# VectorE's row sums three banks behind its multiplies, and its sum of the output halves behind the third multiply of the third K part, in a decode attention kernel

## The chip, the cores and the metric

The kernel runs on one core of one Trainium2 chip. The metric is the device time of one execution in microseconds (us), lower is better. The times are the median of several executions; the profile is one further execution, taken by the hardware profiler.

## What is computed

Two attention blocks, A and B, of one form: one new token per sequence (batch 2), 32 heads of 192 numbers, and a cache of 8192 keys and values per head, all bf16. The outputs of the blocks are joined along the last axis.

```python
q = (x @ wq).reshape(B, Sq, H, Dh).transpose(0, 2, 1, 3)
scores = einsum("bhqd,bhkd->bhqk", q, k_cache) * (Dh ** -0.5)
p = softmax(scores, axis=-1)
o = einsum("bhqk,bhkd->bhqd", p, v_cache)
return o.transpose(0, 2, 1, 3).reshape(B, Sq, H * Dh) @ wo
# x (2, 1, 640), k_cache and v_cache (2, 32, 8192, 192), wq (640, 6144), wo (6144, 640)
```

Every key and value is used once, so the caches are read once from the chip's memory, and there is little arithmetic for each byte.

## The kernel before

**Units and parts.** The work is cut into 16 units (`NU`): a block, a sequence and a group of 8 heads. The keys of a unit are spread over 128 partitions, each with 512 tokens of one head (`TP`), and so are the values. Both are loaded in 3 parts (`NCH`) of 64 KB per partition, 8.39 MB a part. Three buffers in `big` (`NBUF`) hold them in turn. The list `loads` gives the order: K parts 0 to 2 of the first unit, then in turns V part c of unit u-1 and K part c of unit u, and last the three V parts of the last unit. All loads stand in one queue that SyncE issues (`ld_kv`, waits at L504 to L506): load i waits until the load three before it has been used up (`done`, L495), a K part by the last of its sums on TensorE ("sl"), a V part by its last product on TensorE ("pv"). So a K load waits for a "pv", and a V load for an "sl".

**A K part** has 170 whole tokens. VectorE multiplies them in place by the query (`dve_mul`, L303), in 5 instructions (`NSUB`) that are called m0 to m4 here: four of 32 tokens (6144 numbers per partition) and one of 42 (8064). Tokens that are cut by a part's edge are multiplied into `pad` (L301). TensorE then adds the 192 products of a token down to 16 with 12 matmuls against an identity, 32 tokens to a PSUM bank (`pe_sum`, L420, called s0 to s4); there are three such banks, `scps0` to `scps2`, taken in turn (`bank`, L306). VectorE adds the last 16 of a bank (`dve_red`, L311, called r0 to r4) into the scores `sc`. The ten tokens that are over go to a bank of their own (`pe_rest`, L432), which VectorE adds once for a unit (`dve_rest`, L315). A sum s waits for its multiply, and for the r of the bank's user three sums ago (`prev`, L559).

**Softmax.** After the last r of the third part VectorE takes the row maximum, GpSimd the maximum over partitions, ScalarE the exponential, and VectorE spreads the probabilities into `pb` (`dve_spread`, L338).

**A V part** is 85 matmuls of 384 columns and one or two small ones (`pe_pv`, L450 and L456), called pv0 to pv2, all three into the one bank `ops`. Its two halves (tokens of even and odd number) are then added, and divided by the sum of the exponentials: VectorE's reciprocal (L347), copy (L350) and sum (L353), then ScalarE (L356) and one matmul (L462) that places the eight rows. The function `turn_out` records the three steps of VectorE and ScalarE's.

**Order.** The program writes out by hand, unit by unit, what each engine does in which order (`put`, L566, and the loop at L569); each engine goes strictly in its order, and waits of semaphores stand between the engines. Within a unit u and part c, TensorE does pv c of the unit before (v = u - 1), and then s0 to s4 of K part c. VectorE does the multiplies of K part c, with the row sum of the bank before behind each. `turn_out` stands ahead of the third part's multiplies. Unit 0 has no V work, and after the last unit the loop goes once more with V work alone. Units from 1 on run as a hardware loop.

Of the kernel before, what the change touches and what calls it, by code (L numbers as in the profile page):

```python
# [119 lines left out]
def build_kernel(nc, blocks, out):  # L120
# [10 lines left out]
    NCH = 3  # L131
# [5 lines left out]
    NSUB = TC // SUB  # L137
# [18 lines left out]
    with ExitStack() as es:  # L156
# [135 lines left out]
        def dve_su(u):  # L292
            return lambda eng: eng.tensor_tensor(su[:], esel[:], onehot[:, S_dve.at(u)].broadcast_to([128, 144]), ALU.mult)  # L293

        def dve_mul(u, c, k):
            b = buf["k", u, c]

            def fn(eng):
                if k == 0:
                    for t, lo, hi, src in fragments(b, c):  # L300
                        eng.tensor_tensor(pad[:, t, lo:hi], src, qt[:, 0, lo:hi], ALU.mult)  # L301
                t = tokens(b, c, SUB * k, size(k))
                return eng.tensor_tensor(t, t, qt[:].broadcast_to([128, size(k), Dh]), ALU.mult)  # L303
            return fn
# [4 lines left out]
        def dve_red(u, c, k):  # L309
            lo = TC * c + SUB * k  # L310
            return lambda eng: eng.tensor_reduce(sc[:, lo:lo + SUB], scps[bank(u, c, k)][:], AXL.X, ALU.add)  # L311
# [18 lines left out]
        def dve_spread(ranges):  # L330
            dst = pb[:].rearrange("p (g a j h) -> p g a j h", a=2, j=4, h=UH)
            src = sc[:].rearrange("p (g j a) -> p g a j", j=4, a=2)

            def fn(eng):
                for lo, hi in ranges:
                    for a in range(2):
                        shape = [128, hi - lo, 4, UH]
                        ins = eng.tensor_tensor(dst[:, lo:hi, a], src[:, lo:hi, a].unsqueeze(3).broadcast_to(shape),  # L338
                                                mask[:].unsqueeze(1).unsqueeze(1).broadcast_to(shape), ALU.mult)
                return ins  # L340
            return fn
# [73 lines left out]
        def pe_sum(u, c, k):  # L415
            t = tokens(buf["k", u, c], c, SUB * k, SUB)

            def fn(eng):
                for j in range(NJ):
                    ins = eng.matmul(scps[bank(u, c, k)][:], ident[:], t[:, :, j * DG:(j + 1) * DG],  # L420
                                     start=(j == 0), stop=(j == NJ - 1))
                return ins
            return fn

        def pe_rest(u, c):
            t = tokens(buf["k", u, c], c, SUB * NSUB, REST)
            parts = [(REST * c, REST, t)] + ([(NCH * REST, 2, pad[:])] if c == NCH - 1 else [])

            def fn(eng):
                for lo, n, src in parts:  # L430
                    for j in range(NJ):
                        ins = eng.matmul(rest[:, lo:lo + n, :], ident[:], src[:, :, j * DG:(j + 1) * DG],  # L432
                                         start=(j == 0), stop=(j == NJ - 1))
                return ins
            return fn
# [7 lines left out]
        def pe_pv(u, c):  # L443
            b = buf["v", u, c]

            def fn(eng):
                for j in range(TC // 2):
                    j0 = col(TC * c + 2 * j)
                    last = c == NCH - 1 and j == TC // 2 - 1
                    ins = eng.matmul(ops[0:MP, 0:QW], pb[:, j0:j0 + MP],  # L450
                                     bufs[b][:, OFF[c] + j * QW:OFF[c] + (j + 1) * QW],
                                     start=(c == 0 and j == 0), stop=last, skip_group_check=True)
                    if j == 0:
                        for t, lo, hi, src in fragments(b, c):
                            j0 = col(NCH * TC + t)
                            eng.matmul(ops[0:UH, lo:hi], pb[:, j0:j0 + UH], src, start=False, stop=False,  # L456
                                       skip_group_check=True)
                return ins
            return fn

        def pe_pl(u):
            return lambda eng: eng.matmul(oacc_all[:, 0:Dh], place[:, S_pe.at(UH * u, 128, UH)], o_sb[:],  # L462
                                          start=False, stop=True, skip_group_check=True)
# [95 lines left out]
        def prev(u, c, k):  # L559
            n = u * NCH * NSUB + c * NSUB + k - 3  # L560
            return ("r", n // (NCH * NSUB), n // NSUB % NCH, n % NSUB) if n >= 0 else None
# [4 lines left out]
        def put(eng, slot, name, fn, waits, lag=0):  # L566
            slots[eng].setdefault(slot, []).append((name, fn, [w for w in waits if w is not None], lag))

        for u in range(NU + 1):  # L569
            real, old = u < NU, u >= 1  # L570
            v = u - 1

            def red(c, k):
                put("dve", u, ("r", c, k), dve_red(u, c, k), [("s", u, c, k), ("sp", u - 1) if u else None])

            def turn_out():
                put("dve", u, ("rc", -1), dve_rc, [("pv", v, NCH - 1), ("of", v - 1)])
                put("dve", u, ("oh", -1), dve_ohi, [("of", v - 1)])
                put("dve", u, ("os", -1), dve_osum, [("oh", v)])
                put("act", u, ("of", -1), act_of, [("os", v), ("rc", v), ("pl", v - 1)])  # L580

            def v_part(c):
                if c == 0:
                    put("pe", u, ("l", -1), pe_l, [("exp", v), ("sp0", v), ("os", v - 1), ("rc", v - 1)])
                put("pe", u, ("pv", c, -1), pe_pv(v, c), [("v", v, c), ("sp", v) if c else None])

            if not real:
                for c in range(NCH):
                    v_part(c)
                turn_out()  # L590
                put("pe", u, ("pl", -1), pe_pl(v), [("of", v)])
                continue
            put("dve", u, ("su", 1), dve_su(u + 1), [("q", u)])
            for c in range(NCH):
                if old:
                    v_part(c)
                if old and c == NCH - 1:
                    turn_out()
                for k in range(NSUB):
                    w = [("k", u, c), ("qe", u), ("sl", u - 1, NCH - 1) if u and c == 0 else None]  # L600
                    put("dve", u, ("m", c, k), dve_mul(u, c, k), w)
                    put("pe", u, ("s", c, k), pe_sum(u, c, k), [("m", u, c, k), prev(u, c, k)])
                    if old and c == NCH - 1 and k == 0:
                        put("pe", u, ("pl", -1), pe_pl(v), [("of", v)])
                    if k:
                        red(c, k - 1)
                    elif c:
                        red(c - 1, NSUB - 1)
                put("pe", u, ("sl", c), pe_rest(u, c),
                    [("m", u, c, NSUB - 1), ("rl", u - 1) if u and c == 0 else None])  # L610
            c = NCH - 1
            red(c, NSUB - 1)
            put("dve", u, ("rl",), dve_rest, [("sl", u, c)])
            put("dve", u, ("mx",), dve_max, [("rl", u)])
            put("dve", u, ("mp",), dve_mp, [("mx", u), ("ar", u - 1) if u else None, ("negm",)])
            put("dve", u, ("nm",), dve_nm, [("ar", u)])
            put("dve", u, ("nb",), dve_nb, [("nm", u), ("exp", u - 1) if u else None])
            put("pe", u, ("q", 1), pe_q, [("su", u + 1), ("qe", u)])
            put("pool", u, ("ar",), pool_ar, [("mp", u), ("nm", u - 1) if u else None])
            put("act", u, ("qe", 1), act_q, [("q", u + 1), ("m", u, NCH - 1, NSUB - 1)])  # L620
            put("act", u, ("exp",), act_exp, [("nb", u), ("l", v) if u else None])
            g0, g1 = -(-TC // 8), TP // 8
            put("dve", u, ("sp0",), dve_spread([(0, g0), (g1 - 1, g1)]),
                [("exp", u), ("pv", v, NCH - 1) if u else None, ("mask",)])
            put("dve", u, ("sp",), dve_spread([(g0, g1 - 1)]), [])
# [107 lines left out]
```

## Time and profile before

| | |
|---|---|
| median of 3 executions | 1964.3 us |
| the executions | 1964.3, 1970.02 and 1940.62 us |
| the profiled execution | 1947.18 us, its span 1945.5 us |
| mean granted TensorE clock in it | 0.938 of full speed |
| TensorE busy (matmuls) | 1533.6 us, 79% of the span |
| VectorE busy | 1121.8 us, 58% |
| ScalarE, GpSimd busy | 30.1 us, 8.8 us |
| DMA | 836.98 MB, 430 GB/s over the span |

In the lines of the profile, PE is TensorE, PEld its weight loads, DVE VectorE, ACT ScalarE, POOL GpSimd, and SP SyncE, which issues all the loads. A row of the timeline has the start in us, the duration in us, the engine, the line and the operation, its count, and in brackets how long the engine had stood idle before it and what it waited for. A row of the groups has a count, the busy time in us and the mean in ns of one, and the idle time ahead. In a row of the DMA issues the last number is the time in us from issue to landing; it contains the wait behind loads issued earlier. A row of the windows gives the busy us of each engine in that stretch, then the granted clock (PEclk), the busy share of the 16 DMA engines and the bytes moved.

### The profile page before, as it was taken

Reading aid. Unit: us, or ns where it says so; the run is one execution under the profiler, and the core shown is the slowest. Engines: PE = TensorE matmul, PEld = TensorE weight load, DVE = VectorE, ACT = ScalarE, POOL = GpSimd, SP = SyncE. Lnnn points to the kernel's source line nnn. Section 1 sums busy time; section 2 is a strip of 40 time slices with the busy share of each in tenths; the row PEclk is TensorE's granted clock in tenths of the full one; section 3 lists DMA queues with packets and bytes.
Section 4 is the critical chain, followed back from the end, with each engine's and each line's share of the span. In section 5 each row is a group of like instructions: output and inputs, shape, how many; then the busy total and the mean of one; then the engine's idle time right before and its main releaser. Section 6 shows DMA issues by size and latency. Waiting matters only on the chain.

```text
span 1945.5 us, 18505 instructions
## 1 busy us (share of the span) xinstructions
PE 1533.6 (79%) x8255; PEld 780.4 (40%) x8256; DVE 1121.8 (58%) x835; ACT 30.1 (2%) x76; POOL 8.8 (0%) x60
## 2 busy tenths in 40 slices
PE   5678778887977878778787977978788787977979
PEld 3234344333433434344343433434344343433435
DVE  0786555665556475555765557476565656556450
ACT  0000000000000000000000000000000000000000
POOL 0000000000000000000000000000000000000000
PEclk9899889899999989999899999989999998999989
DMA  9999999999999999999999999999999999999998
GB/s 428 433 429 431 429 435 435 433 433 437 424 431 431 431 431 431 431 431 431 434 434 438 433 435 431 434 433 431 433 435 434 434 435 434 433 434 431 431 433 345
DMA packets 15149, 836.98 MB, mean 430 GB/s; under 512 B 1688, under 2 KB 1824, under 8 KB 2208
## 3 DMA queue, kind: packets, MB, share of 16 engines
q1 hardware_dynamic: 15136, 836.78, 99.5%
q8 instruction: 11, 0.18, 0.0%
q14 instruction: 2, 0.02, 0.0%
HBM read 836.77 MB, written 0.01 MB: 430 GB/s over the span
## 4 chain that ended last, share of the span: by engine, by line
PE 54%; DVE 30%; issue 14%; DMA 2%; another core or an unknown queue 0%; POOL 0%; ACT 0%; DVEq 0%; SPq 0%; ACTq 0%; POOLq 0%
PE ops L450 34%; DVE big L303 23%; PE scps L420 16%; DVE sc L311 3%; PE rest L432 2%; DMA big<-in_B_wq_dram 2%; DVE pb L338 1%; PE scps L402 1%; DVE rmax L319 1%; PE outps L484 0%; PE ops L456 0%; PE scps L484 0%; POOL mg L344 0%; DVE o_hi L350 0%
## 5 line engine op out<-in xcount | busy, mean ns | idle before, releaser
L420 PE MATMUL scps<-big,ident 128*128 128x512 bf16 x2880 | 728.5, 410 | 298.7 <-DVE big L303 298.7
L303 DVE TENSOR_TENSOR big<-big,qt 128x6144 bf16<-128x6144 bf16 (+1 forms) x240 | 850.2, 3548 | 0.0
L450 PE MATMUL ops<-big,pb 128*40 128x384 bf16 x4080 | 706.8, 335 | 0.0
L420 PEld LDWEIGHTS scps<-big,ident 128*128 128x128 bf16 x2880 | 281.8, 104 | 729.7 <-DVE big L303 376.6
L450 PEld LDWEIGHTS ops<-big,pb 128*40 128x40 bf16 x4080 | 412.9, 102 | 270.0 <-issue 24.7
L311 DVE TENSOR_REDUCE sc<-scps 128x32 f32<-128x512 f32 x240 | 164.5, 685 | 265.8 <-PE scps L420 265.8
L347 DVE RECIPROCAL rc<-ops 8x1 f32<-8x1 f32 x16 | 2.5, 156 | 322.3 <-PE ops L450 322.3
L301 DVE TENSOR_TENSOR pad<-big,qt 128x128 bf16<-128x128 bf16 (+1 forms) x64 | 11.5, 200 | 135.0 <-DMA big<-in_A_k_cache_dram 68.9
L338 DVE TENSOR_TENSOR pb<-sc,mask 128x704 bf16<-128x704 f32 (+2 forms) x96 | 76.3, 863 | 14.1 <-ACT sc L366 14.1
L438 PE MATMUL ops<-rs,mask 128*8 128x1 f32 x32 | 3.1, 167 | 84.8 <-DVE pb L338 84.8
L432 PE MATMUL rest<-big,ident 128*128 128x160 bf16 x576 | 47.7, 233 | 0.0
L432 PEld LDWEIGHTS rest<-big,ident 128*128 128x128 bf16 x576 | 42.7, 98 | 12.1 <-issue 1.8
L438 PEld LDWEIGHTS ops<-rs,mask 128*8 128x8 f32 x32 | 1.6, 90 | 88.4 <-DVE pb L338 82.8
L402 PE MATMUL scps<-big,pb 128*64 128x384 bf16 x160 | 28.5, 343 | 2.4 <-DMA big<-in_B_wq_dram 1.9
L356 ACT ACTIVATE o_sb<-o_hi,rc 8x192 bf16<-8x192 f32 x16 | 7.3, 454 | 1357.7 <-DVE o_hi L353 1357.7
L402 PEld LDWEIGHTS scps<-big,pb 128*64 128x64 bf16 x160 | 18.4, 116 | 12.3 <-DMA big<-in_B_wq_dram 2.3
L293 DVE TENSOR_TENSOR su<-esel,onehot 128x144 bf16<-128x144 bf16 x17 | 5.1, 301 | 28.7 <-PE outps L410 28.7
L394 PE MATMUL rest<-ident,pb 4*128 4x4 bf16 x5 | 0.4, 178 | 21.5 <-DMA pb<-in_B_x_dram 21.5
L315 DVE TENSOR_REDUCE sc<-rest 128x30 f32<-128x480 f32 x16 | 10.5, 657 | 6.9 <-PE rest L432 6.9
L344 POOL PARTITION_ALL_REDUCE mg<-mp x16 | 5.8, 366 | 1866.9 <-DVE mp L322 1866.9
L359 ACT ACTIVATE qt<-outps 128x192 bf16<-128x192 f32 x17 | 5.6, 330 | 455.6 <-PE outps L410 455.6
L366 ACT ACTIVATE sc<-sc,nb 128x512 f32<-128x512 f32 x16 | 11.5, 721 | 32.8 <-DVE nb L328 32.8
(66 smaller groups left out, 125.6 us busy)
## 6 DMA issues: line engine op xcount, KB each, us to landing
big<-in_B_wq_dram SPq DMA_DIRECT2D x1, 7680.0 KB, 37.2
big<-in_A_wo_dram SPq DMA_DIRECT2D x1, 7680.0 KB, 24.3
big<-in_A_wq_dram SPq DMA_DIRECT2D x1, 7168.0 KB, 20.2
big<-in_B_wo_dram SPq DMA_DIRECT2D x1, 4640.0 KB, 21.2
big<-in_B_wo_dram SPq DMA_DIRECT2D x1, 1760.0 KB, 25.1
big<-in_B_wo_dram SPq DMA_DIRECT2D x1, 800.0 KB, 26.6
big<-in_A_wq_dram SPq DMA_DIRECT2D x1, 512.0 KB, 3.8
big<-in_A_k_cache_dram SPq DMA_DIRECT2D x24, 29.9
```

The source lines that it names most:

```text
L301: eng.tensor_tensor(pad[:, t, lo:hi], src, qt[:, 0, lo:hi], ALU.mult)
L303: return eng.tensor_tensor(t, t, qt[:].broadcast_to([128, size(k), Dh]), ALU.mult)
L311: return lambda eng: eng.tensor_reduce(sc[:, lo:lo + SUB], scps[bank(u, c, k)][:], AXL.X, ALU.add)
L315: eng.tensor_reduce(dst, rest[:, 0:NCH * REST, :].rearrange("p (c t) g -> p c t g", c=NCH), AXL.X, ALU.add)
L319: return eng.tensor_reduce(rmax[:], sc[:], AXL.X, ALU.max)
L338: ins = eng.tensor_tensor(dst[:, lo:hi, a], src[:, lo:hi, a].unsqueeze(3).broadcast_to(shape), mask[:].unsqueeze(1).unsqueeze(1).broadcast ...
L356: return eng.activation(o_sb[:], o_hi[:], ACTF.Identity, scale=rc[:])
L366: return eng.activation(sc[:], sc[:], ACTF.Exp, bias=nb[:], scale=scale, accum_out=rs[:])
L402: ins = eng.matmul(flat[blk][64 * blk:64 * blk + 64, 0:QW], xz[:, blk, c, XM - m:XM - m + 64], wq_t[blk][:, c, QW * m:QW * m + QW], start= ...
L420: ins = eng.matmul(scps[bank(u, c, k)][:], ident[:], t[:, :, j * DG:(j + 1) * DG], start=(j == 0), stop=(j == NJ - 1))
L432: ins = eng.matmul(rest[:, lo:lo + n, :], ident[:], src[:, :, j * DG:(j + 1) * DG], start=(j == 0), stop=(j == NJ - 1))
L450: ins = eng.matmul(ops[0:MP, 0:QW], pb[:, j0:j0 + MP], bufs[b][:, OFF[c] + j * QW:OFF[c] + (j + 1) * QW], start=(c == 0 and j == 0), stop= ...
```

## The change

In the order of VectorE's work three things move; no operation is added or taken away, and nothing is changed in what is computed, in the loads, or in their order.

1. Row sum number n of a unit (n counts its 15 banks) stood behind the multiply n + 1; it now stands behind the multiply n + 3. The last three row sums of a unit stand together behind its last multiply, where one stood alone.
2. `turn_out` (reciprocal, copy and sum of the output halves) stood ahead of the third part's m0; it now stands ahead of its m3, behind the row sum that follows m2.
3. On TensorE the matmul that places the output rows (L462) stood behind s0 of the third part, and now stands behind s3.

```diff
             for c in range(NCH):
                 if old:
                     v_part(c)
-                if old and c == NCH - 1:
-                    turn_out()
                 for k in range(NSUB):
+                    if old and c == NCH - 1 and k == 3:
+                        turn_out()
                     w = [("k", u, c), ("qe", u), ("sl", u - 1, NCH - 1) if u and c == 0 else None]
                     put("dve", u, ("m", c, k), dve_mul(u, c, k), w)
                     put("pe", u, ("s", c, k), pe_sum(u, c, k), [("m", u, c, k), prev(u, c, k)])
-                    if old and c == NCH - 1 and k == 0:
+                    if old and c == NCH - 1 and k == 3:
                         put("pe", u, ("pl", -1), pe_pl(v), [("of", v)])
-                    if k:
-                        red(c, k - 1)
-                    elif c:
-                        red(c - 1, NSUB - 1)
+                    n = NSUB * c + k - 3
+                    if n >= 0:
+                        red(n // NSUB, n % NSUB)
                 put("pe", u, ("sl", c), pe_rest(u, c),
                     [("m", u, c, NSUB - 1), ("rl", u - 1) if u and c == 0 else None])
             c = NCH - 1
-            red(c, NSUB - 1)
+            for k in range(NSUB - 3, NSUB):
+                red(c, k)
```

On VectorE, at the start of a unit (K part 0) in the loop, before; `128x6144` and `128x8064` are multiplies, `sc<-scps0` is the row sum of the first bank, and the rows of L110 compute the number that the next semaphore wait needs:

```order
L303 TENSOR_TENSOR big<-big,qt 128x6144 x2
L110 REGISTER_ALU
L110 ISA
L311 TENSOR_REDUCE sc<-scps0 128x32
L303 TENSOR_TENSOR big<-big,qt 128x6144
L110 REGISTER_ALU
L311 TENSOR_REDUCE sc<-scps1 128x32
L303 TENSOR_TENSOR big<-big,qt 128x6144
L110 REGISTER_ALU
L311 TENSOR_REDUCE sc<-scps2 128x32
L303 TENSOR_TENSOR big<-big,qt 128x8064
```

The same place with the change:

```order
L303 TENSOR_TENSOR big<-big,qt 128x6144 x4
L110 REGISTER_ALU
L110 ISA
L311 TENSOR_REDUCE sc<-scps0 128x32
L303 TENSOR_TENSOR big<-big,qt 128x8064
L110 REGISTER_ALU
L311 TENSOR_REDUCE sc<-scps1 128x32
```

Four multiplies, where there were two, now stand ahead of the first instruction that needs a sum of TensorE's.

On VectorE, at the start of the third K part, before:

```order
L347 RECIPROCAL rc<-ops 8x1
L350 COPY o_hi<-ops 8x192
L110 REGISTER_ALU
L353 TENSOR_TENSOR o_hi<-ops,o_hi 8x192
L301 TENSOR_TENSOR pad<-big,qt 128x128
L303 TENSOR_TENSOR big<-big,qt 128x6144
L311 TENSOR_REDUCE sc<-scps0 128x32
```

With the change, from the third part's m2 on:

```order
L303 TENSOR_TENSOR big<-big,qt 128x6144
L110 REGISTER_ALU
L311 TENSOR_REDUCE sc<-scps0 128x32
L110 REGISTER_ALU
L347 RECIPROCAL rc<-ops 8x1
L350 COPY o_hi<-ops 8x192
L110 REGISTER_ALU
L353 TENSOR_TENSOR o_hi<-ops,o_hi 8x192
L303 TENSOR_TENSOR big<-big,qt 128x6144
L110 REGISTER_ALU
L311 TENSOR_REDUCE sc<-scps1 128x32
L303 TENSOR_TENSOR big<-big,qt 128x8064
```

The reciprocal, which waits for pv2, stood ahead of the part's `pad` and m0, and now stands behind its m2; the row sum ahead of it is that of the last bank of the part before.

On VectorE, from the last multiply of a unit on, with the change (before, one row sum stood behind the one that follows the last multiply, where three stand now):

```order
L303 TENSOR_TENSOR big<-big,qt 128x8064
L110 REGISTER_ALU
L311 TENSOR_REDUCE sc<-scps2 128x32
L110 REGISTER_ALU
L311 TENSOR_REDUCE sc<-scps0 128x32
L110 REGISTER_ALU
L311 TENSOR_REDUCE sc<-scps1 128x32
L110 REGISTER_ALU
L311 TENSOR_REDUCE sc<-scps2 128x32
L110 REGISTER_ALU
L315 TENSOR_REDUCE sc<-rest 128x3x10
```

The last sum on TensorE (s4, in `scps2`) now waits for the first of these four, since it stands in the same bank.

## The prediction

> **What bounds the kernel now.** I read the page's slices and queues first, then the windows, the waits, the DMA issues, and one unit of the timeline.
>
> ```profile
> span 1945.5 us, 18505 instructions
> PE 1533.6 (79%) x8255; PEld 780.4 (40%) x8256; DVE 1121.8 (58%) x835; ACT 30.1 (2%) x76; POOL 8.8 (0%) x60
> DMA  9999999999999999999999999999999999999998
> GB/s 428 433 429 431 429 435 435 433 433 437 424 431 431 431 431 431 431 431 431 434 434 438 433 435 431 434 433 431 433 435 434 434 435 434 433 434 431 431 433 345
> q1 hardware_dynamic: 15136, 836.78, 99.5%
> ```
> ```profile
> 15.00:1915.00 1900.00, 1507.23 (x7986) 765.08 (x7987) 1118.66 (x824) 26.41 (x66) 5.85 (x16) 0.94 1.00 433
> 1938.00:1945.50 7.50, 5.71 (x86) 3.48 (x80) 0.48 (x1) 0.43 (x1) 0.00 (x0) 1.00 0.01 3
> ```
>
> No engine is busy all the time, but the transfers are: between 15 and 1915 us the DMA share is 1.00 at 433 GB/s, and the one queue's packets fill 99.5% of the span. Only the last 7.5 us, the end of the output product and its store, move nothing. The time is the bytes: 836.78 MB at 433 GB/s are 1932.5 us, and a start and an end lie around them. The chain of waits puts most of its shares on TensorE and VectorE, but that tells only who released the last instruction; it isn't a bound while loads are queued.
>
> So the question is whether the queue ever runs dry, and by how little it doesn't. The groups and one unit:
>
> ```profile
> L303 DVE TENSOR_TENSOR big<-big,qt 128x6144 bf16<-128x6144 bf16 x192 | 641.4, 3348 | 0.0
> L303 DVE TENSOR_TENSOR big<-big,qt 128x8064 bf16<-128x8064 bf16 x48 | 208.8, 4349 | 0.0
> L311 DVE TENSOR_REDUCE sc<-scps 128x32 f32<-128x512 f32 x240 | 164.5, 685 | 265.8 <-PE scps L420 265.8
> L347 DVE RECIPROCAL rc<-ops 8x1 f32<-8x1 f32 x16 | 2.5, 156 | 322.3 <-PE ops L450 322.3
> ```
> ```profile
> 1062.82 0.33 SPq L254 DMA_DIRECT2D big<-in_B_v_cache_dram  x1
> 1083.95 0.33 SPq L254 DMA_DIRECT2D big<-in_B_k_cache_dram  x1
> 1086.75 0.69 DVE L311 TENSOR_REDUCE sc<-scps 128x32 f32<-128x512 f32 x1 [8.80 <-PE scps L420]
> 1087.36 3.35 DVE L303 TENSOR_TENSOR big<-big,qt 128x6144 bf16<-128x6144 bf16 x1
> ...
> 1091.23 3.35 DVE L303 TENSOR_TENSOR big<-big,qt 128x6144 bf16<-128x6144 bf16 x1
> ...
> 1107.88 0.29 DVE L301 TENSOR_TENSOR pad<-big,qt 128x64 bf16<-128x64 bf16 x2 [7.83 <-DMA big<-in_B_k_cache_dram]
> ...
> 1117.30 0.33 SPq L254 DMA_DIRECT2D big<-in_B_k_cache_dram  x1
> 1120.01 0.69 DVE L311 TENSOR_REDUCE sc<-scps 128x32 f32<-128x512 f32 x1 [4.70 <-PE scps L420]
> ...
> 1132.75 4.40 PE L420 MATMUL scps<-big,ident 128*128 128x512 bf16 x12 [2.10 <-DVE big L303]
> ...
> 1138.02 0.33 SPq L254 DMA_DIRECT2D big<-in_B_v_cache_dram  x1
> ...
> 1138.34 13.83 PE L450 MATMUL ops<-big,pb 128*40 128x384 bf16 x84
> 1152.20 0.16 DVE L347 RECIPROCAL rc<-ops 8x1 f32<-8x1 f32 x1 [18.90 <-PE ops L450]
> ...
> 1153.05 0.20 DVE L301 TENSOR_TENSOR pad<-big,qt 128x128 bf16<-128x128 bf16 x1
> ...
> 1173.80 2.77 PE L420 MATMUL scps<-big,ident 128*128 128x512 bf16 x12 [2.10 <-DVE big L303]
> ...
> 1177.71 0.33 SPq L254 DMA_DIRECT2D big<-in_B_v_cache_dram  x1
> ...
> 1183.15 0.20 PE L438 MATMUL ops<-rs,mask 128*8 128x1 f32 x2 [5.29 <-DVE pb L338]
> 1199.42 0.33 SPq L254 DMA_DIRECT2D big<-in_B_k_cache_dram  x1
> ```
>
> Two of VectorE's waits are of the kernel's own making. Its row sums stand 265.8 us in all: at 1086.75 and at 1120.01 a row sum waits (8.80 and 4.70 us) until TensorE, busy with a V part, comes to the first sum, and the multiplies behind it wait too. The reciprocal stands 322.3 us: at 1152.20 it has waited 18.90 us for pv2.
>
> What these waits cost the queue is read from when loads are issued. Four of the issues, asked for by time:
>
> ```profile
> big<-in_B_v_cache_dram SPq DMA_DIRECT2D x1, 25.7
> ...
> big<-in_B_k_cache_dram SPq DMA_DIRECT2D x1, 23.9
> ```
> ```profile
> 502.16 0.33 SPq L254 DMA_DIRECT2D big<-in_A_k_cache_dram  x1
> 523.01 0.33 SPq L254 DMA_DIRECT2D big<-in_A_v_cache_dram  x1
> ```
> ```profile
> big<-in_A_k_cache_dram SPq DMA_DIRECT2D x1, 22.6
> ```
> ```profile
> big<-in_A_v_cache_dram SPq DMA_DIRECT2D x1, 21.8
> ```
>
> The V load issued at 1062.82 lands 25.7 us later, at 1088.5. The K load behind it is issued at 1083.95, so 4.6 us before that, and lands at 1107.9, 19.3 us after it: a part takes 19.3 us, and six parts, one unit, 116 us. In the other pair the first lands at 524.8, and the second, issued 1.75 us before, at 544.8: 20.0 us later, so about 0.7 us were lost. From these a load must be issued some 2.45 us (1.75 + 0.7, an estimate) before the one ahead lands. The margin of the unit shown is then 4.6 - 2.45 = 2.1 us in 116. The loop of compute is nearly as long as that of the transfers, but shorter.
>
> **The change, part by part.** No bytes, no instructions of VectorE or TensorE and no matmuls are added or removed; the work moves in order.
>
> *Multiplies ahead of the row sum.* By the rows at 1087.36 and 1091.23 a multiply and a row sum take 3.87 us together. K part 1 lands at 1107.88. With the change, m0, m1 and m2, each with an old row sum that is long ready, begin at 1108.1 and end with their row sums at 1119.7; m3 ends at 1123.0; r0 doesn't wait, since pv1 ends at 1117.3 and s0, 2.8 us long, at 1120.1. m4 ends at about 1127.9 (4.3 us), r1 at 1128.6, and s4, which now waits for r1 in the same bank, begins at 1128.7, where it began at 1132.75. That is 4.0 us earlier; s4 also ran slowly there (4.40 us; 2.77 in the row at 1173.80), so up to 5.6 us. The new wait of s4 costs 0.69 us in each part (one row sum), included here; behind it are only the rest's matmuls and the next pv.
>
> *The output halves behind m2.* K part 2, issued at 1117.30, lands about two parts behind part 1, at 1107.9 + 38.7 = 1146.6. Before, its `pad` begins at 1153.05. With the change the three pairs fill 1146.8 to 1158.4; pv2, some 5 us earlier by the step ahead, has long ended, so the three small steps (0.85 us, 1152.20 to 1153.05) don't wait; m3 with its row sum takes to 1163.1, m4 to 1167.4, r1 to 1168.1. s4 begins at 1168.2, not 1173.80: 5.6 us earlier. r2 and r3 fit under it, r4 follows it as before. What is behind keeps its distances, so pv0 begins at about 1177.6, where it began at 1183.15, and the K load goes out at 1193.8, where it went at 1199.42. Bounds: 6.45 us if nothing else came late (1153.05 - 1146.6), and none at all if VectorE found part 2 landing only after pv2. I take 5.6, as its three pieces are all read from rows.
>
> *The moved matmul of L462* goes from behind s0 to behind s3, and its cost, a quarter of a microsecond on TensorE, stays; ScalarE's step ahead of it ends about 1.1 us after the halves are added, before m3 is done. Nothing waits for it within the unit.
>
> *What all this is worth.* The slack per unit goes from 2.1 to about 7.7 us, and in place of VectorE's waits for TensorE stand waits for landings. No part lands earlier for it while the queue never ran dry. What is won is what did run dry: in the page's slices under 431 GB/s (428, 429, 429, 424; the last apart) 14 of 431 are missing from a slice of 48.6 us, so 1.6 us in all. The lower bound is the 0.7 of the one late load.
>
> [...]
>
> The sum: the profiled execution took 1947.2 us, of which 1945.5 are its span; less 1.6 us that makes **1945.6 us**. The median of the three shown is 1964.3, but they reach from 1940.62 to 1970.02, and the profiled one is among the lower. The forecast says that executions of the changed kernel lie at the transfers' own time. A slower one before would then be one whose loop of compute was longer: 17.1 us above the profiled one (1964.3 - 1947.2) are 1.1 us for each of 15 units with V work, for which the loop must have grown 2.1 + 1.1 = 3.2 us of 116; the changed order holds 7.7.
>
> **Rivals.** *A: the transfers make the spread.* If slower executions are slower because the memory delivers less, the loop of compute has nothing to do with it, and the change nothing to give: about 1964 us, within 1950 to 1972. For it: the trace shown has hardly a gap, so it can't say what a slow one looks like. Against it: the rate between gaps is steady (431 to 438 in nearly all slices), and the margin is just thin enough to be lost.
>
> *B: slower, by TensorE's clock.* The sums now come in bursts, and TensorE stands idle longer between landings:
>
> ```profile
> 1178.00:1182.00 4.00, 0.00 (x0) 0.00 (x0) 2.52 (x7) 1.12 (x3) 0.36 (x1) 0.81 1.10 475
> 1182.00:1186.00 4.00, 2.85 (x11) 1.38 (x12) 4.00 (x7) 0.00 (x0) 0.00 (x0) 0.50 0.99 426
> 1187.00:1199.00 12.00, 12.00 (x74) 7.35 (x73) 5.86 (x2) 0.00 (x0) 0.00 (x0) 0.99 1.01 437
> ```
>
> After an idle stretch (no matmul from 1178 to 1182) the granted clock was 0.50, and 0.99 some microseconds later. If the clock stayed at half through a whole pv0, its 13.8 us would be 27.7, some 12 us above the 16.3 that it takes now with its slow start; that is beyond the 7.7 us by 4.3 us a unit, and 15 units make 65 us: about 2010 us. It decides from about 24 us for pv0 (16.3 + 7.7). Against it: the clock recovers within 4 us. [...]
>
> *C: faster by over 2%.* From 1964.3 that is below 1925.8, less than the bytes take at 433 GB/s with the ends around them; it needs a bad run of before beside a good one of after.
>
> *D: the row sums wait all the same*, now at landings, and sums come no earlier: if K parts landed too late for four multiplies to be done under pv0, the wait of 8.80 us would move and not go. The time would be that of the forecast or 1947.2, as the queue is full either way.
>
> **How the numbers follow.** The forecast, with D in it, has 0.67, its own range 1939 to 1950. A has 0.26, B 0.03, C 0.04. The range, 1938 to 1967, takes in most of A. A measurement of this kernel tells about 2% from no change. Forecast and A are both within it, so within 2% has 0.93; faster by more has C's 0.04, slower by more B's 0.03.
>
> **What the profile after would show.** Right: the share of q1 at 99.5% or above; VectorE's idle time ahead of L311 far under 265.8 us and ahead of L347 near zero, with idle time ahead of L301 on DMA grown well over the present waits; K loads issued some 10 us before the landing ahead, where 4.6 was shown; longer times to landing. All executions would lie near 1945. Wrong: slices with a DMA digit under 9 or under 424 GB/s; a granted clock well under 0.938 with pv0 above 24 us; or executions spread to 1964 as before with the queue full, which would be A.

## The result, and the profile after

The median is 1940.5 us over 20 executions (1940.16 to 1941.10), where the kernel before, in 20 executions beside it, had 1964.28 (1940.39 to 1970.02). The ratio of after to before is 0.9927, with a 95% interval of 0.9899 to 0.9955: 0.7% faster, clear of noise and within the 2% that the forecast spoke of. The profiled execution took 1940.39 us (before 1947.18).

The forecast was 1945.6 us, its own range 1939 to 1950, the whole range 1938 to 1967. More striking than the median is the spread: under 1 us after the change, 30 us before it.

From the page of the changed kernel, the span, the transfer rate per slice, the queue, and three groups (busy us, mean ns, then the idle time ahead and who ended it):

```profile
span 1938.7 us, 18520 instructions
GB/s 416 440 432 434 432 433 434 433 433 433 433 434 433 433 433 433 435 435 433 435 434 433 433 433 433 433 433 434 434 434 434 435 433 434 433 433 433 434 432 381
q1 hardware_dynamic: 15136, 836.78, 99.8%
...
L301 DVE TENSOR_TENSOR pad<-big,qt 128x128 bf16<-128x128 bf16 (+1 forms) x64 | 11.9, 206 | 649.5 <-DMA big<-in_B_k_cache_dram 343.1
L311 DVE TENSOR_REDUCE sc<-scps 128x32 f32<-128x512 f32 x240 | 160.8, 679 | 26.6 <-PE scps L420 26.6
...
L347 DVE RECIPROCAL rc<-ops 8x1 f32<-8x1 f32 x16 | 2.3, 147 | 42.7 <-PE ops L450 42.7
```

From the third slice on, the slices have 432 to 435 GB/s (the last apart); the dip to 424 is gone. VectorE's row sums wait 26.6 us where they waited 265.8. The reciprocal's 42.7 us are one wait, that of the last unit, where VectorE has nothing else to do. What VectorE waits for now is K parts landing, 649.5 us ahead of L301: it is ahead of the transfers.

The first line of section 4 of the two pages, the chain of work that ended last by engine, tells the same; before first, then after:

```profile
PE 54%; DVE 30%; issue 14%; DMA 2%; another core or an unknown queue 0%; POOL 0%; ACT 0%; DVEq 0%; SPq 0%; ACTq 0%; POOLq 0%
```
```profile
DMA 43%; PE 25%; DVE 19%; issue 12%; DVEq 0%; POOL 0%; ACT 0%; SPq 0%; ACTq 0%; POOLq 0%
```

Transfers have 2% of the chain before and 43% after.

One unit of the changed kernel in the timeline, to set beside the unit in the prediction:

```profile
1105.30 0.29 DVE L301 TENSOR_TENSOR pad<-big,qt 128x64 bf16<-128x64 bf16 x2 [19.94 <-DMA big<-in_B_k_cache_dram]
...
1125.98 4.45 PE L420 MATMUL scps<-big,ident 128*128 128x512 bf16 x12 [2.10 <-DVE sc L311]
...
1143.99 0.23 DVE L301 TENSOR_TENSOR pad<-big,qt 128x128 bf16<-128x128 bf16 x1 [18.07 <-DMA big<-in_B_k_cache_dram]
...
1155.74 0.15 DVE L347 RECIPROCAL rc<-ops 8x1 f32<-8x1 f32 x1
...
1165.43 2.76 PE L420 MATMUL scps<-big,ident 128*128 128x512 bf16 x12 [1.92 <-DVE sc L311]
...
1169.35 0.33 SPq L254 DMA_DIRECT2D big<-in_B_v_cache_dram  x1
...
1182.83 13.16 DVE L303 TENSOR_TENSOR big<-big,qt 128x6144 bf16<-128x6144 bf16 x4
1190.62 0.33 SPq L254 DMA_DIRECT2D big<-in_B_k_cache_dram  x1
```
```profile
big<-in_B_v_cache_dram SPq DMA_DIRECT2D x1, 32.7
```

The reciprocal at 1155.74 has no wait ahead of it. The V load issued at 1169.35 lands 32.7 us later, at 1202.0; the K load behind it goes out at 1190.62, 11.4 us before that. In the unit of before that the prediction shows, a K load went out 4.6 us ahead.

### The profile page after: what moved, and what is told of

Read it like the earlier page. It is cut to its first block, busy times and chain, and to the rows that moved or that the text cites. A ratio compares the mean times of both kernels' runs of the same rounds, so it can differ in the third digit from the quotient of the medians.

```text
span 1938.7 us, 18520 instructions
## 1 busy us (share of the span) xinstructions
PE 1518.8 (78%) x8255; PEld 781.2 (40%) x8256; DVE 1118.8 (58%) x835; ACT 30.1 (2%) x76; POOL 8.8 (0%) x60
## 4 chain that ended last, share of the span: by engine, by line
DMA 43%; PE 25%; DVE 19%; issue 12%; DVEq 0%; POOL 0%; ACT 0%; SPq 0%; ACTq 0%; POOLq 0%
DMA big<-in_A_k_cache_dram 20%; DMA big<-in_B_k_cache_dram 19%; PE ops L450 18%; DVE big L303 15%; PE scps L420 4%; DVE sc L311 3%; DMA big<-in_B_wo_dram 2%; PE rest L432 1%; DMA pb<-in_B_x_dram 1%; PE scps L402 1%; DVE pb L338 1%; DVE rmax L319 0%; PE ops L456 0%; POOL mg L344 0%; DVE o_hi L350 0%
## 5 line engine op out<-in xcount | busy, mean ns | idle before, releaser
L420 PE MATMUL scps<-big,ident 128*128 128x512 bf16 x2880 | 713.5, 405 | 305.4 <-DVE sc L311 283.1
L450 PE MATMUL ops<-big,pb 128*40 128x384 bf16 x4080 | 704.0, 334 | 0.0
L420 PEld LDWEIGHTS scps<-big,ident 128*128 128x128 bf16 x2880 | 282.1, 103 | 720.2 <-DVE sc L311 361.1
L450 PEld LDWEIGHTS ops<-big,pb 128*40 128x40 bf16 x4080 | 411.7, 102 | 268.3 <-issue 22.0
L301 DVE TENSOR_TENSOR pad<-big,qt 128x128 bf16<-128x128 bf16 (+1 forms) x64 | 11.9, 206 | 649.5 <-DMA big<-in_B_k_cache_dram 343.1
L311 DVE TENSOR_REDUCE sc<-scps 128x32 f32<-128x512 f32 x240 | 160.8, 679 | 26.6 <-PE scps L420 26.6
L432 PEld LDWEIGHTS rest<-big,ident 128*128 128x128 bf16 x576 | 45.2, 102 | 15.3 <-issue 7.0
L432 PE MATMUL rest<-big,ident 128*128 128x160 bf16 x576 | 49.6, 238 | 0.0
L347 DVE RECIPROCAL rc<-ops 8x1 f32<-8x1 f32 x16 | 2.3, 147 | 42.7 <-PE ops L450 42.7
```

The lines of the kernel that those rows point to most:

```text
L450: ins = eng.matmul(ops[0:MP, 0:QW], pb[:, j0:j0 + MP], bufs[b][:, OFF[c] + j * QW:OFF[c] + (j + 1) * QW], start=(c == 0 and j == 0), stop= ...
```

## Where the 6.8 us between the two profiled executions lie

The last K load, its landing, and the end of the kernel: the issue rows and the times to landing, before and then after.

```profile
1813.62 0.33 SPq L254 DMA_DIRECT2D big<-in_B_k_cache_dram  x1
...
1880.32 15.60 PE L450 MATMUL ops<-big,pb 128*40 128x384 bf16 x85
...
1926.91 8.36 PE L484 MATMUL outps<-big,oT 128*2 128x320 bf16 x96
...
1943.75 0.43 ACT L386 ACTIVATE pb<-scps 2x320 bf16<-2x320 f32 x1 [8.02 <-PE scps L484]
```
```profile
big<-in_B_k_cache_dram SPq DMA_DIRECT2D x1, 29.6
```
```profile
1799.84 0.33 SPq L254 DMA_DIRECT2D big<-in_B_k_cache_dram  x1
...
1872.26 16.69 PE L450 MATMUL ops<-big,pb 128*40 128x384 bf16 x85
...
1919.94 6.68 PE L484 MATMUL outps<-big,oT 128*2 128x320 bf16 x96
...
1929.29 5.89 PE L484 MATMUL scps<-big,oT 128*2 128x320 bf16 x80 [0.83 <-DMA big<-in_B_wo_dram]
1935.44 1.48 PE L484 MATMUL scps<-big,oT 128*2 128x320 bf16 x16 [0.26 <-DMA big<-in_B_wo_dram]
1936.96 0.43 ACT L386 ACTIVATE pb<-scps 2x320 bf16<-2x320 f32 x1 [9.87 <-PE scps L484]
```
```profile
big<-in_B_k_cache_dram SPq DMA_DIRECT2D x1, 40.7
```

The last K part lands at 1843.2 before and at 1840.5 after: the transfers ran dry about 2.7 us less. Before, nearly all of it was lost at five loads that went out 1.8 to 3.6 us ahead of the landing before them. From that landing to the first matmul of the last unit's pv0 it takes 37.1 us before (to 1880.32) and 31.8 after (to 1872.26), 5.3 us less. That is the shortening of the third part which the prediction worked out as 5.6, but here, in the last unit, no further K load stands behind it: three V products and the output product follow on TensorE one after another, and they end the kernel. Together the last pv0 begins 8.1 us earlier, and the last evacuation (L386) 6.8. In between, a slower pv0 (16.69 against 15.60) costs 1.1 us; the first of the two output products gains 1.7 (6.68 against 8.36); and the second ends with 1.9 less of a lead, of which 1.1 are waits for the last pieces of the output weights (0.83 and 0.26), for which TensorE now arrives too early.

This divides the 6.8 us at the landing; it doesn't show that earlier landings alone would have saved 2.7, since the last unit of before follows TensorE's own order of work and not the landing, as is worked out below. Nor is the end of before always longer: its fastest executions (1940.15 to 1940.5 us) are as short as those of the changed kernel.

## The experiments

In all of them before is timed beside. Its executions there lay between 1940 and 1956 us, save one at 2307, with medians of 1945.1 to 1945.7; the group from 1964 to 1970 was seen in the first timing alone. The experiments come from three rounds, each on another chip, and the chip of the first timing isn't on record. So differences of a microsecond between runs of different rounds mean little, and that the long group belongs to one chip isn't ruled out.

**Each part of the change alone.** `e2_lag_only` undoes this of the change (the diff is against the changed kernel):

```diff
+                if old and c == NCH - 1:
+                    turn_out()
                 for k in range(NSUB):
-                    if old and c == NCH - 1 and k == 3:
-                        turn_out()
...
-                    if old and c == NCH - 1 and k == 3:
+                    if old and c == NCH - 1 and k == 0:
                         put("pe", u, ("pl", -1), pe_pl(v), [("of", v)])
```

> Only the row sums move three banks back; the sum of the output halves stays ahead of the third part's first multiply. Theory L, both parts do the same job: part 1's sums end 4 to 5.6 us earlier, so the third V part ends about when the third K part lands and the reciprocal hardly waits; the slack is some 6 to 7 us and all executions lie near 1941. Rival, the reciprocal ahead of the third part is what ties VectorE to TensorE: the slack stays near 2 us and the times stay in two groups, median 1944 to 1965.

Measured 1942.02 us (1940.45 to 1942.23), 0.9969 of before (0.9955 to 0.9984).

`e3_turn_only` undoes the rest:

```diff
-                    n = NSUB * c + k - 3
+                    n = NSUB * c + k - 1
...
-            for k in range(NSUB - 3, NSUB):
-                red(c, k)
+            red(c, NSUB - 1)
```

> Only the sum of the output halves (and its placing matmul) moves behind the third part's third multiply; the row sums stay one multiply behind. Theory L: the third part's multiplies begin at its landing, some 6 us earlier, of which about 1 us goes to the wait for its first sum; slack about 6 us, all executions near 1941. Rival, the row sums are what matters: slack near 2 us, two groups as before, median 1944 to 1965.

Measured 1940.48 us (1940.18 to 1940.89), 0.9972 of before (0.9957 to 0.9987). VectorE's waits in the two, the row sums moved alone and then the output halves alone:

```profile
DVE rc L347 <- PE ops L450: 326.1, 16, 41.3
...
DVE sc L311 <- PE scps L420: 50.6, 25, 3.4
```
```profile
DVE sc L311 <- PE scps L420: 153.7, 51, 8.2
DVE rc L347 <- PE ops L450: 41.7, 1, 41.7
```

Either part takes its own wait away or most of it (the row sums' 265.8 us become 50.6, the reciprocal's 322.3 become the 41.7 of the last unit) and leaves most of the other's, and either is enough to free the transfers. Both rivals, by which only one of the two matters, fell. But the way that was expected for the first did not come: with the row sums moved alone the reciprocal waits 326.1 us, as long as before, and not hardly. What it gains in the first two parts is enough, as it seems. The two do the same job, so their gains don't add: moving the output halves alone has all of it, and the row sums alone all but 1.5 us.

**How much slack there is.** In the next kernels VectorE takes further row maxima of the scores in each unit, into a tile that nothing reads, ahead of the one that counts; they stand in the path from the third K part to pv0. In the trace 8 of them take 4.8 us.

```diff
+        dose = sb("dose", [128, 8], F32)
...
         def dve_max(eng):
+            for i in range(8):
+                eng.tensor_reduce(dose[:, i:i + 1], sc[:], AXL.X, ALU.max)
             return eng.tensor_reduce(rmax[:], sc[:], AXL.X, ALU.max)
```

> The changed kernel with 8 more row maxima of the scores per unit, written to a place that nothing reads, ahead of the one that counts: by the pace of row sums in a row (0.62 us each) some 5 us more in the path from the third K part to the first V product. Theory L: the slack of 8.9 us per unit (loads go out 11.4 us before the landing ahead, less 2.45) holds it: time near 1940.5, issues 6.4 us ahead of the landing instead of 11.4. Theory T: the same time, as nothing but transfers counts. If the slack were used up otherwise: 5 us for each of 16 units, near 2020.

Measured 1943.01 us (1942.33 to 1946.98). The 4.8 us in each of 16 units, 77 us of work, cost 2.5 us in all. Nothing was expected, and a bound by compute would give some 80. In the loop the K loads of the second part go out 5.2 to 5.8 us ahead of the landing, where 6.4 was expected. Two kernels tell where the 2.5 us are, with the same row maxima in all units but the last, and in the last alone. The diff is against the kernel ahead; its last change takes the last unit out of VectorE's hardware loop, so that it can differ:

```diff
-        def dve_max(eng):
-            for i in range(8):
-                eng.tensor_reduce(dose[:, i:i + 1], sc[:], AXL.X, ALU.max)
-            return eng.tensor_reduce(rmax[:], sc[:], AXL.X, ALU.max)
+        def dve_max(u):
+            def fn(eng):
+                for i in range(8 if u < LASTU else 0):
+                    eng.tensor_reduce(dose[:, i:i + 1], sc[:], AXL.X, ALU.max)
+                return eng.tensor_reduce(rmax[:], sc[:], AXL.X, ALU.max)
+            return fn
...
-                S_dve.emit(eng, [(1, NU, 1)])
+                S_dve.emit(eng, [(1, LASTU, 1)])
```

> The changed kernel with the 8 further row maxima (4.8 us in the trace of the run ahead) in all units but the last, whose instructions stand outside the hardware loop. Theory E (what the loop gives is hidden under the transfers, and only the last unit, which has no K loads behind it, ends late): 1940.5, as without them, since the loads still go out 6 us before the landing ahead. Rival, the slack of the loop is smaller than its margins say: 1943, as with the maxima in all units.

Measured 1941.15 us (1940.41 to 1942.74).

> The 8 further row maxima in the last unit alone. Theory E: the whole 2.5 us of the run with maxima in all units come from here, 1943.0; of the 4.8 us some 2.5 go into the wait for the last piece of the output weights, which TensorE had at the end. Rival (the loop's slack): 1940.5.

Measured 1943.53 us (1942.81 to 1944.98), with `u == LASTU` in place of `u < LASTU`. So 15 units swallow 4.8 us each for some 0.6 us in all, and the one last unit passes 3.0 us on. (The two come from another round than the 2.5 us, and with 3.7 us in all add up to it only to about a microsecond.) What lengthens the last unit is paid, and what lengthens the others is not while the slack holds.

**The changed order in the last unit alone.** Against the changed kernel:

```diff
+                lag, at = (3, 3) if u == LASTU else (1, 0)
                 for k in range(NSUB):
-                    if old and c == NCH - 1 and k == 3:
+                    if old and c == NCH - 1 and k == at:
                         turn_out()
...
-                    n = NSUB * c + k - 3
+                    n = NSUB * c + k - lag
...
-            for k in range(NSUB - 3, NSUB):
+            for k in range(NSUB - lag, NSUB):
```

> The order of before in all units but the last, and the changed order in the last. Theory E: the end is up to 5 us earlier than before's, and what the loop loses stays: the times are still spread over several us, the median 2 to 5 us under before's and 1 to 8 us above the changed kernel's 1940.5. Rival, all of the difference between before and after is made in the loop: the times are those of before, 1945 in this chip's runs.

Measured 1943.54 us (1940.46 to 1945.68), 0.9988 of before (0.9977 to 0.9999), and 3.0 us above the changed kernel. The part at the end is there, about 2 us of the median, and the rest belongs to the loop; with an interval that nearly touches 1 the share is not known to better than a microsecond. The trace shows the part at the end more plainly. From the landing of the last K part to the end of the span it takes 97.9 us here (1846.0 to 1944.0) and 98.1 in the changed kernel, but 102.3 in the profile of before and 101.9 in a later one (e11); this execution, the longest of the 12, is long by late landings alone.

**The same row maxima in the kernel before.**

> The kernel before with 8 further row maxima (4.8 us) per unit. Theory L: its slack is about 2.1 us per unit, so some 2.7 us a unit come out over 15 units, 41 us, and up to 5 us at the end: 1980 to 1995; the loads go out less than 2.5 us before the landing ahead. Theory T (the loop of compute doesn't bear on the time): at most the end's 5 us, 1945 to 1952.

Measured 2049.23 us (2048.22 to 2049.60). Theory L's sign is right and its size is not: 103.5 us, where 41 to 46 were expected. Per unit that is 6.9 us from 4.8 us of added work. So something in the loop of before rounds up. The issues of K loads tell by what; first those of before in every second unit, then those of the kernel with 8 further maxima in successive units:

```profile
181.63 0.33 SPq L254 DMA_DIRECT2D big<-in_A_k_cache_dram  x1
...
417.43 0.33 SPq L254 DMA_DIRECT2D big<-in_A_k_cache_dram  x1
...
652.98 0.33 SPq L254 DMA_DIRECT2D big<-in_A_k_cache_dram  x1
...
1316.07 0.33 SPq L254 DMA_DIRECT2D big<-in_B_k_cache_dram  x1
...
1548.17 0.33 SPq L254 DMA_DIRECT2D big<-in_B_k_cache_dram  x1
...
1780.27 0.33 SPq L254 DMA_DIRECT2D big<-in_B_k_cache_dram  x1
```
```profile
1453.17 0.33 SPq L255 DMA_DIRECT2D big<-in_B_k_cache_dram  x1
...
1576.11 0.33 SPq L255 DMA_DIRECT2D big<-in_B_k_cache_dram  x1
...
1699.00 0.33 SPq L255 DMA_DIRECT2D big<-in_B_k_cache_dram  x1
```

And TensorE's granted clock in before, in three stretches that follow each other (PEclk is the third number from the end, ahead of the DMA share and the GB/s):

```profile
1180.50:1187.30 6.80, 4.15 (x15) 2.01 (x16) 6.10 (x9) 0.67 (x2) 0.00 (x0) 0.50 1.07 463
1187.40:1248.70 61.30, 51.87 (x284) 26.79 (x283) 39.41 (x21) 0.00 (x0) 0.00 (x0) 1.00 1.00 432
1248.80:1252.10 3.30, 3.30 (x10) 1.17 (x8) 0.00 (x0) 0.00 (x0) 0.00 (x0) 0.50 1.10 477
```

The clock is at half or at full speed in these stretches. It changes at 1180.48, 1187.31, 1248.75 and 1252.16 us, so they last 6.83, 61.44 and 3.41 us, that is 2, 18 and 1 times one length, 71.68 us for 21. The rest of the trace has the same length: from the clock's first change in it (57.49 us) to its last (1931.41) there are 549 such lengths of 3.4133 us, and every change between lies on this grid to about 1 ns. The changes in the trace of the changed kernel lie on a grid of 3.4133 us too. From here on a window is this length.

Measured in it, before's K loads go out 232.10 us apart over two units: 68 windows are 232.11. Early in the same execution it was 235.80 and then 235.55: 69 windows are 235.52, so the second fits and the first is 0.3 us off. With the row maxima it is 122.88 us a unit in the mean of 14 (single ones 122.6 to 123.1): 36 windows. That before's 232.10 are not the pace of the transfers can be read from the changed kernel: there the loads of the third K part go out 232.20 us apart over two units (1103.22 to 1335.42), which is twelve landings of 19.35 us.

In the unit of before that the prediction shows, the sum at 1132.75, with a granted clock of 0.50 in its first 3.36 us and 1.00 in the rest, took 4.40 us, and the one at 1173.80, at 1.00 throughout, 2.77. So the length of the loop depends on where the windows fall in it. The matmuls of pv0, before, in three successive units show it:

```profile
1183.91 15.48 PE L450 MATMUL ops<-big,pb 128*40 128x384 bf16 x84
...
1301.13 14.91 PE L450 MATMUL ops<-big,pb 128*40 128x384 bf16 x84
...
1416.02 15.48 PE L450 MATMUL ops<-big,pb 128*40 128x384 bf16 x84
```

The same work takes 15.48 and 14.91 us in turns, at a mean granted clock of 0.89 and 0.93, and the units are 116.64 and 115.47 us long in turns: the pattern closes after two units, as 68 windows do. In the changed kernel, whose unit of 116.10 us is 0.05 longer than 34 windows, pv0's matmuls drift instead, from 15.28 us at 246.65 (granted clock 0.90) to 14.93 at 1756.06 (0.92).

That gave a new theory (W): the loop of before feeds itself, and settles at whole windows. It was tried with fewer maxima (4 and 6 in `range`):

> The kernel before with 4 further row maxima (2.4 us) per unit. Theory W (the loop of compute feeds itself, contains no landing, and settles at a length that is a whole number of the clock gate's windows of 3.413 us over one or two units, as the traces show: 68 windows over two units before, 36 over one with 8 maxima): the issues of successive K loads of one part lie 119.5 us apart (35 windows) or, over two units, 69 to 71 windows, 235.5 to 242.3 us; the time between 1965 and 2025 with it, by steps. Rival theory S (the loop grows by what is put into it): from the 2049.2 us with 8 maxima 2.4 us less in 15 units, 2013, a period of 120.5 us, which is no whole number of windows.

Measured 1995.89 us (1994.41 to 1996.66). The issues of one part in successive units:

```profile
1296.71 0.33 SPq L255 DMA_DIRECT2D big<-in_B_k_cache_dram  x1
...
1416.18 0.33 SPq L255 DMA_DIRECT2D big<-in_B_k_cache_dram  x1
...
1535.64 0.33 SPq L255 DMA_DIRECT2D big<-in_B_k_cache_dram  x1
...
1655.11 0.33 SPq L255 DMA_DIRECT2D big<-in_B_k_cache_dram  x1
```

119.47, 119.46 and 119.47 us: 35 windows are 119.47. Theory S's 2013 us and 120.5 us are off. The time lies in W's range, which was wide (1965 to 2025).

> The kernel before with 6 further row maxima (3.6 us) per unit. Theory W: a period of 35.5 or 36 windows, 121.2 or 122.9 us, so about 2023 or 2048. Rival theory S: 2031, with a period of 121.7 us.

Measured 2012.08 us (2011.10 to 2013.70).

```profile
1236.02 0.33 SPq L255 DMA_DIRECT2D big<-in_B_k_cache_dram  x1
...
1357.80 0.33 SPq L255 DMA_DIRECT2D big<-in_B_k_cache_dram  x1
...
1478.83 0.33 SPq L255 DMA_DIRECT2D big<-in_B_k_cache_dram  x1
...
1597.84 0.33 SPq L255 DMA_DIRECT2D big<-in_B_k_cache_dram  x1
```

Over three units 361.82 us, which are 106 windows (361.81), so 35.33 a unit. Any other three units in a row take 361.7 to 361.8 us. Both expectations were off in the size (W's 2023 or 2048, S's 2031): W had looked for whole windows over one or two units, and it is three. The whole number stands, but over three units it was found afterwards and not foretold. From 0 maxima to 4, 6 and 8 the time goes 1945.7, 1995.9, 2012.1, 2049.2 us: 50, 16 and 37 us for 2.4, 1.2 and 1.2 us of work per unit. Steps, not a slope.

**Before once more, and the changed kernel's limit.**

> The kernel before, unchanged, profiled once more. Theory L (the loop of compute is nearly as long as that of the transfers and sometimes longer): the times fall on both sides as they did, near 1941 to 1947 and near 1964 to 1970, and if the profiled execution is a long one, its loads go out less than 2.5 us before the load ahead lands in most units, with gaps of about 1.3 us a unit between landings. Theory T (the transfers make the spread): in a long execution the loads go out as early as before, 4 us or more ahead, and parts take longer than 19.3 us each or one place loses the 20 us at once.

Measured 1946.89 us as the median of 13. Its profile is of an execution of 5387 us, in which the matmuls of L450, L420 and L432 were busy for 5045.8 of the span's 5385.4 us, and it answers neither theory.

> The kernel before, unchanged, profiled once more. Theory W: in a long execution the loads of successive units go out 117.8 us apart on average (69 windows over two units) for many of the units, in a short one 116.05 us (68). Rival, the transfers make the spread: the loads go out early and the landings lie more than 19.4 us apart.

Measured 1944.57 us (1940.39 to 1954.02), and the profiled execution 1948.31, again not a long one. It shows the course of the first profile: 235.8 us over two units at first (119.92 and 115.88), 232.1 later (115.47 and 116.65). So the test was not made: an execution of 1964 to 1970 us was never profiled.

> The changed kernel with 19 further row maxima per unit, 11.6 us. Its slack was 8.9 us by the issue times (11.4 us ahead of the landing, of which 2.45 are needed), so 2.7 us a unit come out over 15 units, 40 us, and some 9 us at the end, where nothing hides them: about 1985 to 1995, more if the loop settles at whole windows here too (119.5 us a unit: 1992 and the end's 9). If the slack is larger than read: 1950.

Measured 2003.21 us (2002.76 to 2004.18). Issues of one part:

```profile
1264.48 0.33 SPq L255 DMA_DIRECT2D big<-in_B_k_cache_dram  x1
...
1383.90 0.33 SPq L255 DMA_DIRECT2D big<-in_B_k_cache_dram  x1
...
1503.37 0.33 SPq L255 DMA_DIRECT2D big<-in_B_k_cache_dram  x1
```

119.42 and 119.47 us, and 119.48 in the mean of 13 units: 35 windows to 0.01 us, though the single units lie between 119.42 and 119.54. Past its slack the changed kernel settles at whole windows as well. 1992 us and the end's 9, 2001 in all, were the second of the two expectations. So the slack lies between 4.8 us (free) and the 11.4 that the 19 maxima take in the trace (not free); it was read as 8.9.

## Why the prediction was right, and where it was off

*What bounds the kernel* held for the changed kernel: the transfers, at 433 GB/s. Its slices show nearly nothing else, and with 4.8 us more work in each of 15 units it still takes 1941.15 us. For before it held only in part. The prediction set the page's chain aside because loads were queued, but the chain, with 2% on transfers, told rightly that TensorE and VectorE released each other there.

*The working of the two moved waits* held to a fraction of a microsecond. From the landing of K part 1 to its s4: 20.8 us predicted (1107.9 to 1128.7), 20.7 measured (1105.30 to 1125.98). From that of part 2: 21.6 predicted (1146.6 to 1168.2), 21.4 measured (1143.99 to 1165.43). K load ahead of the landing before it: 10.8 predicted (1193.8 to 1204.6), 11.4 measured. The new wait of s4 for r1 is there ("DVE sc L311" ends its idle time in both rows) and costs what it was put at. Part 1's s4 is still the slow one (4.45 us), so of its "up to 5.6 us" only the 4.0 came.

*The sum's one term* was mis-sized: 1.6 us predicted, 6.8 measured between the two profiled executions. About 2.7 us of it are the transfers running dry, where the slices had given 1.6; slices of 48.6 us that differ by a few GB/s among themselves are too rough for so little. Nor is the lead of 2.45 us always enough: two loads of before that went out 3.6 us ahead (735.19 and 851.84) still landed 0.6 and 0.8 us late. The other 4.1 are at the end, and there the step failed that treated the end as fixed ("a start and an end lie around them"). The shortened third part is also the last unit's path to the end, where no load hides it. The prediction had the 5.6 us per unit in hand and forgot the one unit that has no successor; e5 and e6 show that this unit alone pays, and e7's trace has the shorter end with the loop of before. So the executions lie at 1940.2 to 1941.1 us, and not near 1945 as was foretold.

*That before's spread is the loop's and not the transfers'* held. Rival A is refuted by the 20 executions within 1 us, and by the kernels with further maxima, whose loop sets their time. But the slack of 2.1 us a unit was a misreading. The working took the loop to contain a landing, and the margin of 4.6 us to be room. In the trace r0 waits 4.70 us for TensorE after part 1 has landed, so that landing isn't in the loop; the loop is pv, sums, row sums and softmax alone, 116.05 us a unit against the transfers' 116.1 (six times 19.35). It had about no slack once it had settled, and in the first units, at 117.8 us, it was the longer of the two and used up the loads' lead. 2.4 us more work cost 3.4 a unit. That the first timing's long executions stayed at 69 windows over two units fits the numbers: in the profiled one that pace ends at about 620 us, and ten more units of 117.8 instead of 116.05 us would add 17 us to its 1947.2, which gives 1964. This is an estimate from that trace; it is argued and not shown.

*Rival B* did not come: pv0 took 15 to 16.7 us, with the granted clock at 0.931 over the span; in the unit of before that the rival was read from, the clock was at full again 4.2 us after the first matmul (1183.15 to 1187.31). Its price was added up wrong, too: 27.7 less 16.3 are 11.4 us and not 12, so it would have been 3.7 us a unit and about 2000 us. *Rival C* neither. *D* neither: the row sums' wait is all but gone (26.6 us).

## What to carry to other kernels

Where transfers bound a kernel, look at how long before the landing ahead each load goes out, and whether the loop that frees the buffers has a landing in it at all: if it hasn't, as here, it runs at its own length (116.05 us a unit beside the transfers' 116.1), and a margin seen in one unit (4.6 us) is no slack. Here the page's chain, with hardly any transfers in it, told this although the queue looked full. Order each engine so that what it can do without another engine's answer stands ahead of what needs one; that may change little in the fastest execution (here 1940.39 to 1940.16 us) and still take the slow ones away (the longest went from 1970.02 to 1941.10). And cost a shortened path in the last round by itself: there nothing is left to hide it (of 4.8 us more work the last unit passed 3.0 on, and 15 units before it some 0.6 in all).

## What the runs showed of the hardware that was not expected

The loop of these kernels settled, where the transfers didn't hold it, at a length that is a whole number of the windows of 3.4133 us on whose grid the granted clock changes: 68 over two units (232.10 us), 35 and 36 over one (119.47 and 122.88), 106 over three (361.8), and 69 over two in passing (235.55). Added work then cost steps: 50 us for 2.4 us a unit, 16 for the next 1.2, and 37 for the 1.2 after that. That the clock's phase does it (by how much work runs at half clock, as pv0's 15.48 us at a granted 0.89 and 14.91 at 0.93 show) is the reading that fits; a run that shifts the phase alone was not made.
